# Four smaller input loads around the first weight columns, two products in token halves, and a re-made instruction order

## The chip, the cores and the metric

The kernel runs on one core of one Trainium2 chip. The metric is device time in microseconds (us), the median of three runs. A profile of one execution is also given; its span runs from the first to the last instruction, and its device time contains some 1.7 us more than the span.

## The reference

The input x has 2048 tokens of 512 bf16 values. Two branches are computed from it and mixed by a gate that depends on the token:

```python
def _A_ref(x, wqkv, wo):          # 32 heads of 16, window W = 256
    q, k, v = qkv[0], qkv[1], qkv[2]
    scores = jnp.einsum("bhqd,bhkd->bhqk", q, k) * (Dh ** -0.5)
    mask = (idx[:, None] - idx[None, :] >= 0) & (idx[:, None] - idx[None, :] < W)
    p = _softmax(jnp.where(mask[None, None], scores, -1e9), axis=-1)
    return o_of(p, v) @ wo
...
def _B_ref(x, w1, w3, w2):        # F = 1376
    return (_silu(x @ w1) * (x @ w3)) @ w2
...
g = _sigmoid((x * gate_w).sum(-1, keepdims=True))
return g * a + (1 - g) * b
```

`o_of` stands for the product of the probabilities with v. So there is a sliding-window attention with its four projections, a gated feed-forward network, and the mix.

## The kernel before

**Tiling.** Everything lies in on-chip memory. x is needed with its 512 features on the partitions: `xT`, in four feature blocks of 128, over 2048 tokens. Tokens are worked in four blocks of 512 (`tcb` or `tq`, 0 to 3). The attention takes the heads in four groups of eight (`c`, 0 to 3). For each group and each key tile of 128 tokens, `main_batch` makes scores with matmuls that use 32 rows of the array each, four beside each other (line 661, "row form"); `edge_batch` does the same for the parts of the window at the edges (line 711). ScalarE takes the exponential (lines 665 and 715), GpSimd cuts it to the window (lines 670, 675 and 728), and `pv` multiplies by v with matmuls that use 32 columns each, four beside each other (line 801, "column form"). All other matmuls use the whole array ("full form"): the q, k and v projections (lines 553 and 606), w1 and w3 (line 967), w2 (line 1026, and line 1082 for the last 128 tokens), and the output projection (line 1055).

**The opening.** The function `opening` (line 422) writes the start out by hand. `constants` makes the identity. `warm_up(WARM)` (line 420) sends 30 matmuls on constants, whose results nobody reads. Then loads are issued on two queues, SyncE's (SP) and ScalarE's (ACT): x's tokens 0 to 255 on SP, tokens 256 to 511 on ACT (line 394), then w1's first 256 columns, half of the rows on SP and half on ACT (line 406). After a table load and `gate_w` on ACT, SP goes on with the first columns of k, w3, q and v, then more of w1 and w3. The remaining three quarters of x come as transposing loads (`turn_x`, line 399) on SP, in order between the later weights.

The first 512 tokens are turned on TensorE instead: four tiles of 128 tokens, four transposes each (line 493), evicted to `xT` by VectorE for tiles 0, 1 and 3 (line 498) and by ScalarE for tile 2 (line 500). A short `warm_up(2)` is planned with the turns. Then the first product of w1 (f = 0, 128 of the 1376 columns, token block 0) runs in two token halves (lines 997 and 999): its first half needs tiles 0 and 1 alone, its second half tiles 2 and 3 too. The k and q projections of the first block are split in the same way (lines 560 and 561). Every other w1 product, f = 1 among them, waits for all four tiles, and also for `last_up`, which is the w3 product of the f before it (line 994).

**The order.** After the opening, the order of all instructions is made by a planner at build time. Each piece of work is an `add(engine, duration, function, dependencies, due, ...)`. `Plan.emit` runs a simulation with these durations: it takes the engine that can start first and, of what could start there, the piece with the smallest due time. The order in which the pieces are taken is the order in which the instructions are written into the engines' queues. At run time each engine goes through its queue in that order and waits where an input is late. The due times come from a table `K` of some 25 numbers (`T0`, `TA`, `PV`, `SEP` and so on) plus a number for each piece, `SHIFT[n]`, where n counts the calls of `add`. The constants `landed` (line 453) tell the planner when each early load will have arrived. Two further numbers in `K`, `ADJ` and `SEP`, change the due times of work in row or column form, depending on the form that TensorE is in.

There are four single PSUM banks (`ch`) for full-form and column-form work, and one block of four banks (`su`) for the scores.

Of the kernel before, what the change touches and what calls it, by code (L numbers as in the profile page):

```python
# [262 lines left out]
def kernel(  # L263
# [12 lines left out]
    nc = tc.nc  # L276
# [17 lines left out]
    VW = DH + 1  # L294
    HALF = (0, 1, 2, 3, 4)
    SCALE = float(DH) ** -0.5
    WARM = 30

    pp = ctx.enter_context(tc.tile_pool(name="pp", bufs=1))
    ps = ctx.enter_context(tc.tile_pool(name="ps", bufs=1, space=bass.MemoryType.PSUM))  # L300
# [47 lines left out]
    add = plan.add  # L348
# [113 lines left out]
    x_in = [arrive(u) for u in landed["x"]]  # L462
# [671 lines left out]
```

## Time and profile before

| | |
|---|---|
| device time, median of 3 runs | 235.06 us |
| the three runs | 234.85, 235.06, 235.82 us |
| device time of the profiled execution | 235.33 us |
| its span | 233.6 us |
| TensorE busy (share of the span) | 225.2 us (96%) |
| VectorE busy | 181.7 us (78%) |
| ScalarE busy | 181.9 us (78%) |
| GpSimd busy | 152.8 us (65%) |
| data moved by DMA | 11.57 MB |

In the rows, PE is TensorE's matmul side and PEld its weight loads, DVE is VectorE, ACT is ScalarE, POOL is GpSimd, and SPq and ACTq are the DMA queues of SyncE and ScalarE. A row of the timeline has its start and its length in us, then engine, line and operation, the tile written and the tile read, and in brackets the idle time before it with what ended it. Rows that follow each other closely are merged, with "x8" for eight of them. Matmuls overlap: one with 512 columns is shown some 380 ns long, though the next starts earlier than that; what a matmul costs is therefore read from the starts.

### The profile page before, as it was taken

The numbers are of one execution on the slowest core, as the hardware profiler recorded it, in microseconds if no ns is written. First come the engines' busy times: TensorE is split into PE (matmuls) and PEld (weight loads), VectorE is DVE, ScalarE is ACT, GpSimd is POOL, SyncE is SP. The second block draws the span as 40 slices with busy tenths as digits, with TensorE's granted clock in tenths as the row PEclk, the third lists the DMA queues.
The fourth block names the chain that finished last, engine by engine and source line by source line (L and its number), as shares of the span: only waits on it lengthen the run. The fifth ranks groups of instructions, "written<-read, shape, count | busy, mean of one in ns | idle before, by whom it ended". The sixth has DMA issues, their size and how long they took to land.

```text
span 233.6 us, 8254 instructions
## 1 busy us (share of the span) xinstructions
PE 225.2 (96%) x3596; PEld 115.9 (50%) x3635; DVE 181.7 (78%) x317; ACT 181.9 (78%) x165; POOL 152.8 (65%) x245
## 2 busy tenths in 40 slices
PE   7999999999999999999999999999999999999995
PEld 7545545634544345545547353535444355455543
DVE  5457777993798869987878787887986779997864
ACT  3479999797778998878998989887968998867310
POOL 7135999576877964749865869567679856654300
DMA  6997701800004000000003000000000000140202
GB/s 188 322 183 196 93 1 21 225 27 1 6 4 133 3 11 14 3 3 3 4 12 81 25 1 3 3 3 0 4 3 3 0 3 18 34 145 20 91 7 84
DMA packets 20653, 11.57 MB, mean 50 GB/s; under 512 B 10025, under 2 KB 20617, under 8 KB 20617
## 3 DMA queue, kind: packets, MB, share of 16 engines
q1 hardware_dynamic: 19920, 10.62, 19.5%
q8 instruction: 28, 0.46, 0.8%
q10 hardware_dynamic: 696, 0.43, 0.6%
q14 instruction: 9, 0.07, 0.1%
HBM read 6.85 MB, written 2.10 MB: 38 GB/s over the span
## 4 chain that ended last, share of the span: by engine, by line
PE 89%; DMA 4%; SPq 2%; issue 2%; DVE 2%
PE ch L967 30%; PE ch L1026 16%; PE ch L553 11%; PE ch L801 9%; PE su L661 8%; PE ch L606 6%; PE ch L1055 6%; PE su L711 2%; DMA xT<-in_A_x_dram 2%; SPq L399 2%; DMA xs<-in_A_x_dram 2%; PE ch L1082 1%; PE ch L904 1%; SPq L406 1%; DVE bsb L1030 0%
## 5 line engine op out<-in xcount | busy, mean ns | idle before, releaser
L665 ACT ACTIVATE Em<-su 128x2048 bf16<-128x2048 f32 x60 | 112.7, 1878 | 22.5 <-PE su L661 20.9
L967 PE MATMUL ch<-xT,w_sb 128*128 128x512 bf16 (+1 forms) x304 | 77.0, 377 | 2.7 <-issue 1.7
L675 POOL TENSOR_SCALAR_AFFINE_SELECT Em<-Em 64x512 bf16<-64x512 bf16 x56 | 37.8, 674 | 26.2 <-ACT Em L665 24.5
L670 POOL TENSOR_SCALAR_AFFINE_SELECT Em<-Em 64x512 bf16<-64x512 bf16 x60 | 40.5, 676 | 18.0 <-ACT Em L665 16.0
L728 POOL TENSOR_SCALAR_AFFINE_SELECT Ee<-Ee 64x1024 bf16<-64x1024 bf16 x32 | 39.5, 1233 | 11.4 <-ACT Ee L715 10.3
L967 PEld LDWEIGHTS <-w_sb 128*128 128x128 bf16 x324 | 28.7, 98 | 32.8 <-issue 4.7
L981 DVE SCALAR_TENSOR_TENSOR h<-tt,ch 128x512 bf16<-128x512 bf16 (+1 forms) x44 | 29.7, 679 | 12.9 <-ACT tt L977 12.6
L1026 PE MATMUL ch<-w_sb,hT 128*128 128x512 bf16 x143 | 37.0, 380 | 0.8 <-issue 0.6
L553 PE MATMUL ch<-xT,wqkv_sb 128*128 128x512 bf16 (+1 forms) x126 | 33.5, 367 | 0.6 <-issue 0.3
L715 ACT ACTIVATE Ee<-su 128x2048 bf16<-128x2048 f32 x16 | 30.1, 1880 | 5.0 <-PE su L711 5.0
L642 POOL COPY vs<-vs 64x256 bf16<-64x256 bf16 x64 | 28.9, 452 | 7.5 <-DVE vs L630 3.1
L987 DVE SCALAR_TENSOR_TENSOR hT<-h,ch 128x512 bf16<-128x512 bf16 x40 | 27.1, 682 | 5.4 <-PE ch L967 3.3
L977 ACT ACTIVATE tt<-ch 128x512 bf16<-128x512 f32 (+1 forms) x44 | 26.1, 598 | 3.9 <-PE ch L967 3.1
L801 PEld LDWEIGHTS <-vs 128*17 128x17 bf16 x1664 | 20.5, 92 | 5.8 <-issue 4.5
L801 PE MATMUL ch<-Em,vs 128*17 128x256 bf16 (+2 forms) x672 | 22.6, 242 | 0.0
L801 PE MATMUL ch<-Ee,vs 128*17 128x64 bf16 x992 | 22.1, 193 | 0.0
L1026 PEld LDWEIGHTS <-hT 128*128 128x128 bf16 x150 | 13.5, 98 | 16.4 <-issue 2.5
L553 PEld LDWEIGHTS <-wqkv_sb 128*128 128x128 bf16 x136 | 12.0, 97 | 13.3 <-issue 2.7
L606 PE MATMUL ch<-wqkv_sb,xT 128*128 128x256 bf16 x128 | 17.2, 273 | 0.2 <-issue 0.2
L661 PE MATMUL su<-qT,kz 32*128 32x256 bf16 x240 | 17.3, 278 | 0.0
L661 PE MATMUL su<-qT,k 32*128 32x256 bf16 x240 | 16.6, 268 | 0.0
L661 PEld LDWEIGHTS <-kz 32*128 32x128 bf16 x240 | 6.0, 91 | 21.2 <-issue 20.8
(83 smaller groups left out, 251.9 us busy)
## 6 DMA issues: line engine op xcount, KB each, us to landing
out_dram<-ot SPq DMA_DIRECT2D x15, 128.0 KB, 1.7
wqkv_sb<-in_A_wqkv_dram SPq DMA_DIRECT2D x6, 256.0 KB, 4.5
w_sb<-in_B_w_dram SPq DMA_DIRECT2D x2, 608.0 KB, 4.8
w_sb<-in_B_w_dram SPq DMA_DIRECT2D x3, 384.0 KB, 3.8
w_sb<-in_B_w_dram SPq DMA_DIRECT2D x2, 512.0 KB, 6.5
wo_sb<-in_A_wo_dram SPq DMA_DIRECT2D x4, 128.0 KB, 3.2
xs<-in_A_x_dram ACTq DMA_DIRECT2D x1, 256.0 KB, 3.8
xs<-in_A_x_dram SPq DMA_DIRECT2D x1, 256.0 KB, 3.5
```

The source lines that it names most:

```text
L553: nc.tensor.matmul(pst[:, t0:t1], lhsT=wqkv_sb[:, dc, col + c * P:col + (c + 1) * P], rhs=xT[:, dc, tq * 512 + t0:tq * 512 + t1], start=(d ...
L606: nc.tensor.matmul(ch[vj.at["ch"]][:, (m - m0) * 2 * P:(m - m0 + 1) * 2 * P], lhsT=xT[:, dc, m * P:(m + 1) * P], rhs=wqkv_sb[:, dc, 2 * D ...
L661: nc.tensor.matmul(su[:, s, a * 256:(a + 1) * 256], lhsT=head_keys(r, t, a), rhs=qT[r, q0:q0 + 256], start=True, stop=True)
L665: nc.scalar.activation(out=Em[job.at["Em"]][:], in_=su[:].rearrange("p s (a q) -> p s a q", a=2), func=ACT.Exp, scale=SCALE)
L670: nc.gpsimd.affine_select(out=e, in_=e, pattern=[[0, 8], [1, KB]], compare_op=ALU.is_ge, fill=0.0, base=0, channel_multiplier=-1)
L675: nc.gpsimd.affine_select(out=e, in_=e, pattern=[[0, 8], [-1, KB]], compare_op=ALU.is_ge, fill=0.0, base=-1, channel_multiplier=1)
L715: nc.scalar.activation(out=Ee[ej.at["Ee"]][:].rearrange("p s t k q -> p s (t k q)"), in_=su[:], func=ACT.Exp, scale=SCALE)
L728: nc.gpsimd.affine_select(out=e, in_=e, pattern=[[0, 4], [0, 4], [1, KB]], compare_op=ALU.is_ge, fill=0.0, base=0, channel_multiplier=-1)
L801: nc.tensor.matmul(po[32 * s:32 * s + VW, lo - 512 * w:hi - 512 * w], lhsT=vs[:, i, a * VW:(a + 1) * VW], rhs=mov, start=(n == 0), stop=(n ...
L967: nc.tensor.matmul(ch[job.at["ch"]][:, t0:t1], lhsT=wA[:, dc, :] if joint else w[:, dc, f * P:(f + 1) * P], rhs=xT[:, dc, tcb * 512 + t0:t ...
L981: nc.vector.scalar_tensor_tensor(out=h1[job.at["h1"]][ru, :], in0=tt[job.at["tt"]][rg, :], scalar=1.0, in1=ch[job.at["ch"]][rg, :], op0=AL ...
L1026: nc.tensor.matmul(bps[:], lhsT=ht[:, mm * P:(mm + 1) * P], rhs=w2_sb[0:fs, f, :], start=(f == 0), stop=(f == NFC - 1))
```

## The change

Loads of x: four of one tile each (128 KB). Tiles 0 and 1 come first, on SP and ACT, then w1's first columns on both queues, then tiles 2 and 3 on both. The 30 matmuls of the warm-up become 23. The product of w1 with f = 1 in token block 0 is now also made in two token halves, and it no longer depends on the w3 product of f = 0. The planner is given other landing times for the early loads, and other durations for the turns (0.43 us for the first two tiles, 0.23 us for the others, in place of 0.36 us for each).

All numbers in `K` are replaced, and the whole of `SHIFT` too. As f = 1 is two calls of `add` in place of four, the list has 1516 numbers in place of 1518. The median size of a number in it is 6.1 in place of 45.3. What the order of the instructions is after this is not to be read from the diff: it comes out of the planner.

```diff
 SHIFT = [
-    0, 0, 0, 0, 0, 0, 0, 0, 0, 0, 0, 0, 0, 0, 0, 0, 0, 143.67, 103.37, 60.03, 88, 142.21, 38.94, 42.12, -2.51, 57.41,
...
+    1.81, 79.34, 55.8, 47.5, 3.69, 40.28, 95.35, 10.12, -10.19, -9.12, 8.12, 0, 0.19, 12.25, 5.26, 32.25,
 ]
...
-    WARM = 30
+    WARM = 23
...
-    K = {"T0": 1.021, "TA": 175.674, "TF0": -5.614, "TF1": 219.201, "PV": -22.302, "EDGE": -2.04, "HOLD": -6.16, "LEAD": -1.713, "QLEAD": -2.523, "V": 9.16, "O0": 9.293, "O1": -5.39, "O2": 6.658, "O3": 32.037, "FE": 0.855, "PE": 8.645, "VE": -2.133, "MK": 65.837, "UP": 4.276, "_km": 1.0, "_lo": 1.0, "LE": 1.877, "ADJ": 7.677, "SEP": -19.643, "BE": 5.555, "OE": 1.299, "END": 5.842}
+    K = {"T0": 2.597, "TA": 171.79, "TF0": -2.088, "TF1": 212.023, "PV": -31.637, "EDGE": -1.998, "HOLD": -4.505, "LEAD": -3.245, "QLEAD": -5.562, "V": 7.957, "O0": 10.94, "O1": -1.559, "O2": 13.899, "O3": 33.228, "FE": 3.405, "PE": 4.943, "VE": -3.088, "MK": 50.721, "UP": 7.032, "_km": 1.0, "_lo": 1.0, "LE": -0.98, "ADJ": 3.157, "SEP": -29.885, "BE": 7.725, "OE": 8.717, "END": 4.513}
...
-        load_x(0, 2, nc.sync)
-        load_x(2, 4, nc.scalar)
+        load_x(0, 1, nc.sync)
+        load_x(1, 2, nc.scalar)
         load_w(w1_sb, B_w1, 0, 2 * P, True)
+        load_x(2, 3, nc.sync)
+        load_x(3, 4, nc.scalar)
...
-    landed = {"x": [3.6, 3.6, 4.4, 4.4, 14.5, 20.6], "w13": [5.25, 7.45, 10.8, 16.6, 12.2, 18.8],
-              "qkv": [6.5, 8.3, 9.1], "gw": 8.0}
+    landed = {"x": [3.65, 3.8, 5.5, 5.8, 14.5, 20.8], "w13": [4.6, 7.7, 10.8, 16.6, 12.2, 18.8],
+              "qkv": [6.85, 8.6, 9.45], "gw": 8.0}
...
-        a = add("PE", 0.36, tr, [x_in[m]], 0.1 * m, take=[(job, "ch")])
+        a = add("PE", 0.43 if m < 2 else 0.23, tr, [x_in[m]], 0.1 * m, take=[(job, "ch")])
...
-            if tcb or f:
+            if tcb or f > 1:
                 a = plan.pieces(HALF, 0.2155, lambda lo, hi, half=half, job=job: half(job, w1_sb, lo, hi),
                                 xt_ready[tcb] + win + last_up + (w_ab if joint else []), due, [(job, "ch")])
             else:
```

191 rows, old and new, of the table SHIFT are left out of this document.

## The prediction

> **What bounds the kernel now.** I read the page's busy shares and its chain of waits first, then the timeline of TensorE (PE), then the opening closely.
>
> ```profile
> span 233.6 us, 8254 instructions
> ...
> PE 225.2 (96%) x3596; PEld 115.9 (50%) x3635; DVE 181.7 (78%) x317; ACT 181.9 (78%) x165; POOL 152.8 (65%) x245
> ...
> PE 89%; DMA 4%; SPq 2%; issue 2%; DVE 2%
> ```
>
> PE is busy 96% of the span and holds 89% of the chain. The order of work matters only as far as it makes PE wait, or makes it change its form. What PE's time consists of shows where steps are followed by starts:
>
> ```profile
> 50.94 2.33 PE L1026 MATMUL ch<-w_sb,hT 128*128 128x512 bf16 x10
> 53.20 0.29 PE L661 MATMUL su<-qT,kz 32*128 32x256 bf16 x4
> 53.32 0.28 PE L661 MATMUL su<-qT,k 32*128 32x256 bf16 x4
> 53.53 0.82 PE L1026 MATMUL ch<-w_sb,hT 128*128 128x512 bf16 x2
> ...
> 20.81 0.41 PE L711 MATMUL su<-qT,kz 32*128 32x64 bf16 x32
> 21.15 0.61 PE L606 MATMUL ch<-wqkv_sb,xT 128*128 128x256 bf16 x4
> ...
> 22.25 1.47 PE L606 MATMUL ch<-wqkv_sb,xT 128*128 128x256 bf16 x12
> ...
> 195.00 0.21 PE L801 MATMUL ch<-Em,vs 128*17 128x64 bf16 x4
> ...
> 196.33 0.20 PE L801 MATMUL ch<-Ee,vs 128*17 128x64 bf16 x4
> 196.46 0.29 PE L661 MATMUL su<-qT,kz 32*128 32x256 bf16 x4
> ...
> L967 PEld LDWEIGHTS <-w_sb 128*128 128x128 bf16 x324 | 28.7, 98 | 32.8 <-issue 4.7
> L967 PE MATMUL ch<-xT,w_sb 128*128 128x512 bf16 (+1 forms) x304 | 77.0, 377 | 2.7 <-issue 1.7
> ```
>
> Ten w2 matmuls and what lies around them: one is shown 0.38 long, so the step is (2.33 - 0.38)/9 = 0.217 us, and ten take 2.17. The row batch starts 2.26 after the first, so 0.09 to 0.10 goes into the change of form. The batch holds PE 0.33 until the next full matmul; 0.33 less some 0.22 of streaming is a second change. I take 0.105 a change. A matmul with 256 columns costs (1.47 - 0.27)/11 = 0.109. A column group takes 1.36 (195.00 to 196.33 and 0.03 for the last), then 0.10 to the row batch beside it.
>
> The loops give the counts: 336 matmuls of 512 columns for w1 and w3, 176 for w2 (the last 11 in parts), 128 for k and q, 64 for the output: 704 x 0.217 = 152.8. 128 for v at 0.109 are 14.0; the tail columns of line 904 about 2.0; 60 row batches at 0.22 are 13.2; 16 edge batches (20.81 to 21.15, less one change) at 0.24 are 3.8; 16 column groups 20.2 (those at the ends of the window are shorter). Together 206.0. In the timeline I count 172 changes of form: 76 row batches and 17 column stretches would have 186, but 14 times a row batch stands beside a column group, as at 196.46, and one change is saved. 172 x 0.105 = 18.1. The sum is 224.1.
>
> ```profile
> 5.58 1.07 PE L967 MATMUL ch<-xT,w_sb 128*128 128x256 bf16 x8
> ...
> 230.56 0.22 PE L1082 MATMUL ch<-w_sb,hX 96*128 96x128 bf16 x1
> ```
>
> From the first product at 5.58 to the last at 230.6 there are 225.0 us. So **at most about 1 us of waiting is left** between them. The waits of 0.16 that the groups put down to "issue" are mostly no waits: line 967 has 324 weight loads but 304 matmuls, so the record of a first matmul is missing where the idle time is shown. Outside lie 5.58 us of opening and some 3 us of last eviction and store, which the change leaves.
>
> **The opening now.**
>
> ```profile
> 0.82 0.46 SPq L394 DMA_DIRECT2D xs<-in_A_x_dram  x1
> ...
> 6.42 6.68 SPq L399 DMA_TRANSPOSE xT<-in_A_x_dram  x4
> ...
> SPq L406 <- DMA xs<-in_A_x_dram: 1.2, 1, 1.2
> ...
> xs<-in_A_x_dram ACTq DMA_DIRECT2D x1, 256.0 KB, 3.8
> xs<-in_A_x_dram SPq DMA_DIRECT2D x1, 256.0 KB, 3.5
> ...
> 1.50:3.30 1.80, 1.80 (x20) 1.80 (x18) 1.58 (x4) 1.41 (x2) 1.58 (x9) 1.00 0.67 151
> 1.50:4.00 2.50, 2.50 (x26) 2.35 (x23) 1.87 (x5) 1.49 (x2) 2.17 (x12) 1.00 0.79 212
> 1.50:4.85 3.35, 3.04 (x35) 2.86 (x33) 1.94 (x6) 1.49 (x2) 2.96 (x14) 1.00 0.87 236
> ...
> 0.85 3.17 PE L420 MATMUL su<-const-bfloat16-1.0 128*128 128x128 bf16 x30 [0.85 <-PEq L1118]
> ...
> 4.34 0.62 PE L493 MATMUL ch<-ident,xs 128*128 128x128 bf16 x8 [0.31 <-DMA xs<-in_A_x_dram]
> 4.78 1.21 DVE L498 COPY xT<-ch 128x512 bf16<-128x512 bf16 x3 [1.15 <-PE ch L493]
> 5.33 0.59 ACT L500 COPY xT<-ch 128x512 bf16<-128x512 bf16 x1 [1.96 <-PE ch L493]
> 6.80 1.04 PE L553 MATMUL ch<-xT,wqkv_sb 128*128 128x256 bf16 x8 [0.15 <-issue]
> 7.68 1.03 PE L967 MATMUL ch<-xT,w_sb 128*128 128x512 bf16 x4
> 8.54 1.25 PE L553 MATMUL ch<-xT,wqkv_sb 128*128 128x256 bf16 x9
> ```
>
> x lands at 4.3 (SP) and 4.6 (ACT), and its first half product starts 1.25 after the former. By 8.54 three products are done: w1 and w3 of f = 0, and k. The last number of a windows row is GB/s: 1.8 us at 151 are 272 KB by 3.30, 2.5 at 212 are 530 KB by 4.00, 3.35 at 236 are 791 KB by 4.85. Since x has 524 KB, a load is seen 0.3 to 0.65 us after its last byte moved.
>
> **The change, part by part.**
>
> *Loads.* The bytes come in the order 262 KB (tiles 0, 1), 262 KB (w1), 262 KB (tiles 2, 3). With the delay just found, tiles 0 and 1 are seen at 3.6 to 3.95, w1 at 4.3 to 4.65, tiles 2 and 3 at 5.15 to 5.5. The first half product then starts at 3.6 + 1.25 = 4.85 at best; at 3.95 and 0.2 more for a turn at the slow clock of the warm-up it is 5.4. I take 5.1, 0.48 earlier than now. It and the first half of f = 1, 0.44 each (the k row: eight halves in 0.88), fill PE to 6.0. Turns of tiles 2 and 3 come between or behind, then evictions of 0.42 on DVE and 0.59 on ACT: 1.0 to 1.35 after landing, so 6.15 to 6.85; I take 6.55. Second halves until 7.4, then k (0.88) until 8.3. Again three products are done, at 8.3 in place of 8.54: **-0.25 us**. The early bounds give 6.15 + 1.75 = 7.9, a gain of 0.6; the late ones 6.85 + 1.75 = 8.6 and 0.2 for k's load arriving behind, a loss of 0.3. The move gains little: tiles 2 and 3 pay for what tiles 0 and 1 win. I count the last of the three as worth its whole difference, since PE has work without a break afterwards.
>
> *Queues.* SP and ACT issue one load more each, 0.46 to 0.5. On SP k, w3 and q come that much later; the sixth load already stood 1.2 waiting for x, which covers it for v and everything behind, the transposing loads at 6.42 among them. If that cover fails, the 0.5 reaches the second token block's data. On ACT the table load and `gate_w` move by 0.5; ACT's first eviction is at 5.33, so nothing waits. Cost 0; bounds 0 and 0.5.
>
> *Warm-up.* Seven fewer matmuls lie beside the loads and save nothing, PE waits for x there. *f = 1 in halves*: 0.88 for 0.87, **+0.01**; its four further weight loads lie beside matmuls (PEld is 50% busy).
>
> *Order.* Nothing in the trace shows the new one. Bounds: the 1 us of waiting can go, and a column group can have a row batch on both sides (34 contacts for 14, 20 x 0.105 = 2.1), so -3.1. On the other side all 14 contacts lost are +1.5, and waits can grow by, say, the 0.15 seen before the k product at 6.80, at each of the 16 column groups: 2.4, together +3.9. Contacts I take as they are. Waits can fall by 1 and rise without such a floor, so I take **+0.4**, nearer to the present 1 us than to the far end.
>
> The sum is 235.33 (profiled) - 0.25 + 0.01 + 0.4 = 235.5. The profiled execution lay 0.27 above the median of 235.06, so I forecast **235.2 us**.
>
> *The clock.* The granted clock reads 1.00 in every window above, yet the durations tell more:
>
> ```profile
> L420 PEld LDWEIGHTS <-const-bfloat16-1.0 128*128 128x128 bf16 x24 | 2.5, 144 | 0.8 <-issue 0.8
> ...
> L493 PEld LDWEIGHTS <-xs 128*128 128x128 bf16 x16 | 0.9, 98 | 0.5 <-DMA xs<-in_A_x_dram 0.5
> ```
>
> Before 3.2 a weight load took 144 ns, from 4.1 on 98; the warm-up's steps of some 0.107 halve only for the last few of the 30, near 3.6. Twenty-three such steps end at about 3.3, ahead of that moment. The Trainium skill ("TensorE: Matmul & The Clock Gate", Part 1) says that the array starts at half clock and that release takes about 3.4 us of sustained activity, in time and not in matmuls; the trace agrees in kind, with some 2.75 us from the first matmul. By that rule the shorter warm-up may miss its window; what this does is the third rival.
>
> **The rivals.**
>
> 1. *The order is tighter* (22%). With 8 more contacts (-0.84), half the waiting gone (-0.5) and the opening's -0.25 the time is 233.5. For it: the search had fresh numbers everywhere. Against: only 1 us is left to win in waits.
> 2. *Column groups ahead of their masks* (30%), the slower side. `pv` needs the last row batch's scores, its exponential and its mask:
>
> ```profile
> 216.30 0.29 PE L661 MATMUL su<-qT,kz 32*128 32x256 bf16 x4
> ...
> 216.75 1.88 ACT L665 ACTIVATE Em<-su 128x2048 bf16<-128x2048 f32 x1 [1.68 <-PE su L661]
> 218.69 0.66 POOL L670 TENSOR_SCALAR_AFFINE_SELECT Em<-Em 64x512 bf16<-64x512 bf16 x1 [1.20 <-ACT Em L665]
> 219.11 0.21 PE L801 MATMUL ch<-Em,vs 128*17 128x64 bf16 x4
> ```
>
>    Here the column group starts 2.8 after the batch, with its mask just in time. PE goes through its queue in order, so a group placed sooner holds up everything. 0.13 at each of 16 groups is 2.1 us, and 235.06 - 0.25 + 2.1 = 236.9. It decides from 0.09 a group (1.43 in all, 1.18 above the median). For it: `PV` and `SEP` make these groups due earlier, -31.6 for -22.3 and -29.9 for -19.6. Against: the planner places nothing before its inputs are planned ready.
> 3. *The change doesn't bring the first products forward* (10%): the clock stays low through them for a second stretch of 2.75, to 6.35. Both first halves take near double, second halves start at some 7.5, three products are done at 9.3, 0.75 late. With the order's 0.4 that is 236.2, half of this case on either side of the border.
>
> **How the numbers follow.** My forecast has 38%. A measurement of this kernel tells about 0.5% from no change, that is 233.9 to 236.2. Faster is the first rival, 0.22; slower the second and half the third, 0.35; the forecast and the rest are 0.43. The likeliest case alone holds 234.2 to 236.2; the range 233.3 to 237.2 takes in the rivals' times.
>
> **What would show it.** Right: the first w1 matmul near 5.1, second halves near 6.55, PE ending 225 us after its start, 172 changes give or take five. Wrong: line 420 weight loads staying at 144 ns and line 493's too (the clock); a first row of line 801 with idle time ahead of it and GpSimd as its releaser (second rival); clearly fewer changes of form (first).

## The result and the profile after

The changed kernel takes 237.45 us (median of 6 runs, 236.90 to 238.94), the kernel before, run beside it, 235.17 us (6 runs, 234.85 to 235.88). The ratio is 1.0104, with an interval of 1.0066 to 1.0141: about 1% slower, where 235.2 and a range up to 237.2 were forecast. The profiled execution took 237.75 us.

From its page, the busy shares:

```profile
span 236.0 us, 8308 instructions
...
PE 230.2 (98%) x3632; PEld 116.5 (49%) x3632; DVE 184.7 (78%) x317; ACT 181.7 (77%) x165; POOL 153.6 (65%) x245
```

TensorE seems 5 us busier, 98% for 96%. That is not a cause: the page of before lacks 39 matmul records (3596 beside 3635 weight loads), and a matmul that is followed at once by another overlaps it. The starts have to be read. The last matmul starts at 232.92, in place of 230.56: 2.36 us later.

**The opening.** TensorE's timeline of the changed kernel (start and length in us, line, tiles, idle time before):

```profile
3.60 1.03 PE L480 MATMUL ch<-ident,xs 128*128 128x128 bf16 x8
4.43 0.42 PE L405 MATMUL su<-const-bfloat16-1.0 128*128 128x128 bf16 x2
5.15 0.73 PE L954 MATMUL ch<-xT,w_sb 128*128 128x256 bf16 x4 [0.30 <-DVE xT L485]
6.14 0.65 PE L480 MATMUL ch<-ident,xs 128*128 128x128 bf16 x8 [0.26 <-DMA xs<-in_A_x_dram]
6.63 0.60 PE L954 MATMUL ch<-xT,w_sb 128*128 128x256 bf16 x4
7.21 1.03 PE L540 MATMUL ch<-xT,wqkv_sb 128*128 128x256 bf16 x8
8.08 0.60 PE L954 MATMUL ch<-xT,w_sb 128*128 128x256 bf16 x4
8.61 0.17 PE L502 MATMUL ch<-ident,gwr 4*128 4x4 bf16 x1
8.72 1.55 PE L954 MATMUL ch<-xT,w_sb 128*128 128x256 bf16 x8
```

The first product starts at 5.15, close to the forecast. But one half product (4 matmuls) later TensorE stands still, until tiles 2 and 3 arrive for their turns at 6.14. Four half products for w1 and k follow, the one at 6.63 still a first half: tile 3 is evicted only at 7.25. The sixth half, which makes three products, begins at 8.72 and is done four matmuls of 0.109 later, at 9.16. Without the small gate product at 8.61, which the kernel before makes only at 9.94, that is 9.05. Before, three products were done at 8.54. So the opening loses 0.5 us.

The pieces of the chain of waits show what TensorE waited for, and the table of DMA issues gives the times from issue to landing:

```profile
1.74 4.61 DMA xs<-in_A_x_dram
...
10.20 5.82 DMA xT<-in_A_x_dram
```

```profile
wo_sb<-in_A_wo_dram SPq DMA_DIRECT2D x4, 128.0 KB, 2.7
xs<-in_A_x_dram SPq DMA_DIRECT2D x2, 128.0 KB, 3.6
xs<-in_A_x_dram ACTq DMA_DIRECT2D x2, 128.0 KB, 4.6
```

Tile 3 was issued at 1.74 and was there at 6.35; 5.15 to 5.5 was forecast. By 4.85 us 828 KB had moved (3.35 us at 247 GB/s), more than the forecast's 791 KB, but by then only 493 of the 512 packets of x had started; the last one of tile 3 ended at 5.79. The first weights of k landed 0.55 later than before (7.08 for 6.53), and TensorE waited some 0.15 for them. The transposing load of the next 512 tokens landed at 16.02 (15.92 before), and there the new order holds a k product that needs it:

```profile
15.11 0.59 PE L540 MATMUL ch<-xT,wqkv_sb 128*128 128x512 bf16 x2
16.07 0.38 PE L540 MATMUL ch<-xT,wqkv_sb 128*128 128x512 bf16 x1 [0.37 <-DMA xT<-in_A_x_dram]
```

Two matmuls cost 0.43, so of the 0.96 between the starts 0.53 is a wait. The kernel before waits at this landing too, for 0.22: its matmul at 15.96 starts 0.44 after the one ahead.

**Two waits for VectorE.** The timelines of several engines near 115 and near 220:

```profile
113.26 2.43 POOL L715 TENSOR_SCALAR_AFFINE_SELECT Ee<-Ee 64x1024 bf16<-64x1024 bf16 x2 [0.98 <-ACT Ee L702]
...
114.60 1.36 DVE L725 TENSOR_TENSOR Ee<-Ee,mlast 128x512 bf16<-128x512 bf16 x1
...
115.66 0.82 PE L540 MATMUL ch<-xT,wqkv_sb 128*128 128x512 bf16 x3
...
115.88 0.74 DVE L1017 TENSOR_SCALAR bsb<-ch,omg 128x512 bf16<-128x512 f32 x1
...
116.67 0.60 PE L593 MATMUL ch<-wqkv_sb,xT 128*128 128x256 bf16 x4 [0.19 <-DVE bsb L1017]
...
217.82 2.43 POOL L715 TENSOR_SCALAR_AFFINE_SELECT Ee<-Ee 64x1024 bf16<-64x1024 bf16 x2 [1.50 <-ACT Ee L702]
...
219.16 1.36 DVE L725 TENSOR_TENSOR Ee<-Ee,mlast 128x512 bf16<-128x512 bf16 x1
...
220.22 0.61 PE L1069 MATMUL ch<-w_sb,hT 128*128 128x128 bf16 x8
...
220.45 0.74 DVE L1046 SCALAR_TENSOR_TENSOR ot<-ch,gq,bsb 128x512 bf16<-128x512 f32 x1
...
221.24 0.21 PE L788 MATMUL ch<-Em,vs 128*17 128x64 bf16 x4 [0.40 <-DVE ot L1046]
```

TensorE wants to begin a new product in a `ch` bank, and waits for VectorE to have read the bank's last content (lines 1017 and 1046 are named as releasers). VectorE comes late, because ahead of that in its queue stands line 725, the second mask of a last edge batch, which takes 1.36 us. It starts 0.13 after the second of GpSimd's two masks there (line 715). From 115.66 to 116.67 stand three matmuls of 0.217, so 1.01 - 0.65 = 0.36 is lost. The second wait is 0.48 (from 220.22 to 221.24 are 1.02; the same eight matmuls and the change of form take 0.54 in the experiment below where VectorE is in time). Together 0.84.

The same instruction in both kernels, all four executions of it with shortest, median and longest time in ns (first row after, second row before):

```profile
L725 DVE TENSOR_TENSOR Ee<-Ee,mlast x4: 411/884/1360, 72.9 to 219.2; 128x512 bf16<-128x512 bf16 x4
```

```profile
L738 DVE TENSOR_TENSOR Ee<-Ee,mlast x4: 411/614/1360, 64.4 to 217.7; 128x512 bf16<-128x512 bf16 x4
```

It took 1.36 us once before as well (at 64.43, 0.30 after a mask of GpSimd had started), and no row of TensorE shows a wait behind it. In these rows it is not enough that the other engine works beside it; what differs is which starts first. In the changed kernel near 73 us VectorE started 0.02 ahead; it took 0.41, and the mask of GpSimd took 0.91, where most of that line take 0.65. Near the end of the kernel before it fell behind GpSimd's mask and took 0.41 too. Two rows of the changed kernel, then two of the kernel before:

```profile
72.94 0.41 DVE L725 TENSOR_TENSOR Ee<-Ee,mlast 128x512 bf16<-128x512 bf16 x1
72.96 0.91 POOL L662 TENSOR_SCALAR_AFFINE_SELECT Em<-Em 64x512 bf16<-64x512 bf16 x1 [0.21 <-ACT Em L652]
...
216.35 1.15 POOL L728 TENSOR_SCALAR_AFFINE_SELECT Ee<-Ee 64x1024 bf16<-64x1024 bf16 x1
...
217.69 0.41 DVE L738 TENSOR_TENSOR Ee<-Ee,mlast 128x512 bf16<-128x512 bf16 x1
```

**Changes of form.** Counted in the timeline as before: 175 for 172 (11 contacts of row batch and column group for 14), 3 x 0.105 = 0.3 us.

**One wait without a name.** Inside an edge batch:

```profile
45.70 0.41 PE L698 MATMUL su<-qT,kz 32*128 32x64 bf16 x31
46.44 0.20 PE L698 MATMUL su<-qT,kz 32*128 32x64 bf16 x1 [0.33 <-issue]
46.57 0.60 PE L954 MATMUL ch<-xT,w_sb 128*128 128x512 bf16 x2
```

The batch takes 0.87 to the next full matmul, where 0.34 is usual. No semaphore is named. Whether this belongs to the change is a question for the experiments.

### The profile page after: what moved, and what is told of

It reads as the page before. It is cut to its first block, busy times and chain, and to the rows that moved or that the text cites. A ratio compares the mean times of both kernels' runs of the same rounds, so it can differ in the third digit from the quotient of the medians.

```text
span 236.0 us, 8308 instructions
## 1 busy us (share of the span) xinstructions
PE 230.2 (98%) x3632; PEld 116.5 (49%) x3632; DVE 184.7 (78%) x317; ACT 181.7 (77%) x165; POOL 153.6 (65%) x245
## 4 chain that ended last, share of the span: by engine, by line
PE 89%; DMA 4%; DVE 2%; SPq 2%; ACT 1%; issue 1%; ACTq 0%
PE ch L954 30%; PE ch L1013 15%; PE ch L540 11%; PE ch L788 9%; PE su L648 8%; PE ch L1042 6%; PE ch L593 5%; DMA xT<-in_A_x_dram 2%; PE su L698 2%; DMA xs<-in_A_x_dram 2%; SPq L384 1%; PE ch L891 1%; PE ch L1069 1%; ACT Em L652 1%; DVE bsb L1017 1%
## 5 line engine op out<-in xcount | busy, mean ns | idle before, releaser
L954 PE MATMUL ch<-xT,w_sb 128*128 128x512 bf16 (+1 forms) x328 | 80.4, 376 | 0.3 <-DVE xT L485 0.3
L715 POOL TENSOR_SCALAR_AFFINE_SELECT Ee<-Ee 64x1024 bf16<-64x1024 bf16 x32 | 40.3, 1258 | 12.5 <-ACT Ee L702 11.3
L954 PEld LDWEIGHTS <-w_sb 128*128 128x128 bf16 x328 | 29.3, 98 | 33.7 <-issue 6.1
L1013 PE MATMUL ch<-w_sb,hT 128*128 128x512 bf16 x150 | 38.4, 380 | 0.0
L629 POOL COPY vs<-vs 64x256 bf16<-64x256 bf16 x64 | 28.3, 442 | 13.8 <-DVE vs L603 8.6
L540 PE MATMUL ch<-xT,wqkv_sb 128*128 128x512 bf16 (+1 forms) x136 | 34.0, 367 | 0.4 <-DMA xT<-in_A_x_dram 0.4
L1017 DVE TENSOR_SCALAR bsb<-ch,omg 128x512 bf16<-128x512 f32 x15 | 11.2, 746 | 8.6 <-PE ch L1013 8.5
```

What stands on the lines that cost most here:

```text
L540: nc.tensor.matmul(pst[:, t0:t1], lhsT=wqkv_sb[:, dc, col + c * P:col + (c + 1) * P], rhs=xT[:, dc, tq * 512 + t0:tq * 512 + t1], start=(d ...
L715: nc.gpsimd.affine_select(out=e, in_=e, pattern=[[0, 4], [0, 4], [1, KB]], compare_op=ALU.is_ge, fill=0.0, base=0, channel_multiplier=-1)
L954: nc.tensor.matmul(ch[job.at["ch"]][:, t0:t1], lhsT=wA[:, dc, :] if joint else w[:, dc, f * P:(f + 1) * P], rhs=xT[:, dc, tcb * 512 + t0:t ...
L1013: nc.tensor.matmul(bps[:], lhsT=ht[:, mm * P:(mm + 1) * P], rhs=w2_sb[0:fs, f, :], start=(f == 0), stop=(f == NFC - 1))
```

## The experiments

The expectations say themselves what each of their theories holds. Each group of runs has its own runs of the kernel before beside it on the same chip.

**1. The loads alone, the order alone.** The kernel before with the new loads and 23 warm-up matmuls, its order untouched:

```diff
-    WARM = 30
+    WARM = 23
-        load_x(0, 2, nc.sync)
-        load_x(2, 4, nc.scalar)
+        load_x(0, 1, nc.sync)
+        load_x(1, 2, nc.scalar)
         load_w(w1_sb, B_w1, 0, 2 * P, True)
+        load_x(2, 3, nc.sync)
+        load_x(3, 4, nc.scalar)
```

> The kernel before with the four-piece loads and 23 warm-up matmuls alone; its planner's numbers, and so its order, stay. Theory A (the new loads are a loss by themselves, and the end moves by what the opening loses): TensorE's queue has the turns of tiles 2 and 3 ahead of the first product, they land near 6.1 us in place of 4.6, so the first product starts near 6.6 in place of 5.58 and the end is 0.9 to 1.1 us later, about 236.2. Rival B (the opening has slack, the loss is all in the order behind it): the end moves by less than 0.3 us.

Measured: 237.3 us (235.74 to 238.87, 10 runs) beside 235.12 (21 runs), ratio 1.0088 [1.0058, 1.0118]. The timeline of TensorE:

```profile
6.20 0.62 PE L495 MATMUL ch<-ident,xs 128*128 128x128 bf16 x8 [1.33 <-DMA xs<-in_A_x_dram]
6.66 1.29 PE L969 MATMUL ch<-xT,w_sb 128*128 128x256 bf16 x8
```

In the old order all turns stand ahead of the first product, so the late tiles 2 and 3 delay it from 5.58 to 6.66. The new loads with the short warm-up are a loss by themselves; in the opening the halves of f = 1 and the new order win part of it back. Theory A's 236.2 fits the profiled execution (236.09, its last matmul 0.74 later than before) and not the median: the 23 warm-up matmuls, run 5, are part of this run. What the loads cost without them no run shows alone.

The reverse, the changed kernel with the old loads and 30 warm-up matmuls:

> The changed kernel with x in two pieces ahead of w1 and 30 warm-up matmuls again; order and halves as in the changed kernel. Theory A: the wait of 0.42 us ahead of the turns of tiles 2 and 3 goes, the first product starts near 5.6 in place of 5.15, the last of the four halves ends about 0.4 earlier; but the wait for the transposed load near 16 us grows by most of that, so the end is 0.1 to 0.4 earlier than the changed kernel. Rival B: no difference. Rival C (the loads are the whole loss): back to within 0.5 us of the kernel before.

Measured: 236.87 us (236.50 to 237.73, 6 runs), ratio 1.0076 [1.0055, 1.0097]. Both waits for VectorE are in its trace, 0.36 and 0.48. So most of the loss is there without the new loads: **it lies in the order.** The two halves of the change don't add up (2.18 and 1.75 against 2.28 together), since either one by itself already makes the start late: tiles 2 and 3 are turned at 6.20 in the one and at 6.03 in the other, for 4.91 before.

**2. The bank waits.** The changed kernel, with the two masks of a last edge batch made in one instruction, from a tile that holds both patterns:

```diff
+    mfull = pp.tile([P, 4, KB], BF16, name="mfull")
...
-            full = 2 if last else 4
...
-            if last:
-                e = Ee[ej.at["Ee"]][:, :, 2:4, 1, :]
...
+            mb = (mfull[:][:, None, :, :].to_broadcast([P, 4, 4, KB]) if last
+                  else medge[:, 1][:, None, None, :].to_broadcast([P, 4, 4, KB]))
+            nc.vector.tensor_tensor(out=e, in0=e, in1=mb, op=ALU.min)
```

> The changed kernel with VectorE's masks of the last edge batch of each head group joined into one instruction, from a mask tile made in the opening; the order stays. In the changed kernel's profile the second of the two instructions took 1.36 us in two of four cases, and VectorE then freed a PSUM bank late for TensorE near 116 and 221 us (waits of 0.35 and 0.47). Theory A (the loss is a sum of separate waits): both waits go or shrink, the end is 0.5 to 0.8 us earlier than the changed kernel. Rival D (the waits are symptoms of a pace set elsewhere, and TensorE loses the time again further on): the two waits go, but the end moves by less than 0.2 us.

Measured: 236.01 us (235.47 to 238.04, 12 runs), ratio 1.0046 [1.0028, 1.0065]; the last matmul starts at 231.10. The timeline near 220:

```profile
217.22 1.00 DVE L728 TENSOR_TENSOR Ee<-Ee,mfull 128x1024 bf16<-128x1024 bf16 x1
...
218.15 0.74 DVE L1048 SCALAR_TENSOR_TENSOR ot<-ch,gq,bsb 128x512 bf16<-128x512 f32 x1
...
218.94 0.61 PE L1071 MATMUL ch<-w_sb,hT 128*128 128x128 bf16 x8
...
219.48 0.21 PE L790 MATMUL ch<-Em,vs 128*17 128x64 bf16 x4
```

One instruction of 1.00 replaces 0.73 and 1.36, VectorE frees its bank in time, and both waits are gone. The median falls by 1.44 us, more than the 0.84 seen in the trace; the intervals of the two ratios (1.0066 to 1.0141, and 1.0028 to 1.0065) leave room for the difference. Since both kernels run the same order, their matmuls can be set side by side. The last one is 1.82 earlier than in the first profile of the changed kernel: 0.41 of it is there by 16 us, 0.52 comes in the edge batch near 46 that is shown above, and 0.36 and 0.48 at the two waits. The latter two are the repair; the others vary from one execution to the next (run 7).

**3. The wait for the second token block.** Four matmuls of the k product near 15 moved behind a score batch and two matmuls of w3:

```diff
+        grp = [r for r in order if r[1].seq in (73, 74, 75, 76)]
+        order[:] = [r for r in order if r[1].seq not in (73, 74, 75, 76)]
+        i = [r[1].seq for r in order].index(828) + 1
+        order[i:i] = grp
```

> The changed kernel with the four matmuls of one projection of the second token block, which wait 0.53 us near 16 us for the transposed load, placed behind a score batch and two matmuls of w3. Theory A: the wait goes, everything behind is about 0.5 us earlier, the end 0.4 to 0.5 us earlier. Rival D: the wait goes, the step comes back at a later wait and the end moves by less than 0.2 us.

Measured: 237.16 us (236.62 to 237.43, 6 runs), ratio 1.0081 [1.0061, 1.0101]. The 0.53 is gone, but in the timeline the score batch behind it now waits for ScalarE's exponential instead:

```profile
15.37 0.29 PE L652 MATMUL su<-qT,kz 32*128 32x256 bf16 x4 [0.32 <-ACT Em L656]
```

The last matmul starts at 232.13, as in the further executions of the changed kernel (232.11 and 232.24, run 7). This wait covers another; it is not a cost that can be taken out alone.

**4. The repairs together.** The changed kernel with the old loads, 30 warm-up matmuls, one mask, and the first half product of f = 1 moved behind the turns of tiles 2 and 3:

```diff
+        grp = [r for r in order if r[1].seq in (813,)]
...
+        i = [r[1].seq for r in order].index(41) + 1
+        order[i:i] = grp
```

> The changed kernel's order with x in two pieces and 30 warm-up matmuls, the edge mask in one instruction, and the turns of tiles 2 and 3 ahead of the first product again. new_order_old_loads ended 1.67 us behind the kernel before in the profiles: 0.83 are the two waits for a bank, 0.45 the turns inside, 0.3 three more changes of form. Theory A (separate waits, nothing comes back): 1.67 - 0.83 - 0.45 = 0.4 us above the kernel before, 235.3 to 235.8. Rival D (lost again further on): 236.3 or more.

Measured: 235.59 us (235.31 to 236.89, 12 runs) beside 235.38 (28 runs), ratio 1.0020 [1.0004, 1.0036]. The timeline:

```profile
5.10 0.61 PE L488 MATMUL ch<-ident,xs 128*128 128x128 bf16 x8
5.64 1.03 PE L958 MATMUL ch<-xT,w_sb 128*128 128x256 bf16 x8
```

The turns of tiles 2 and 3 stand at 5.10 again, and the first two half products follow without a break. With the repairs the new order is nearly as good as the old one: in its profiled execution the last matmul starts at 230.58, 0.02 later than before. It still has the 175 changes of form, 0.3 more, but three products are done at 8.35, counted without the gate product as above (0.19 earlier than before), and the landing of the second token block is no longer waited for. No run tried the changes of form alone. Nothing in it beats the kernel before.

**5. The warm-up.** The kernel before with `WARM = 23`, with nothing else changed:

> The kernel before with 23 warm-up matmuls in place of 30, nothing else. In the profiles so far the last weight load at half clock lies between 3.6 and 5.5 us and the runs with the new loads scatter over 2 to 3 us (before: 1). Theory E (with TensorE less busy in the first microseconds, its clock opens a stretch later in some executions): the median rises by 0.3 to 1.0 us and the runs scatter over more than 1.5 us. Rival F (the scatter comes from the landings of the four pieces, the warm-up has cover): the median stays within 0.3 us of the kernel before and the runs within about 1 us.

Measured: 236.65 us (234.86 to 237.59, 10 runs), ratio 1.0045 [1.0018, 1.0073]. A term that I had put at nothing costs 1.27 us in the median, and the runs lie 2.7 us apart where those of the kernel before lie 1.5 apart. The profiled execution was a short one, 235.26. With 8 warm-up matmuls:

> The kernel before with 8 warm-up matmuls: TensorE is idle from about 1.9 to 4.3 us. Theory E: the last weight load at half clock (over 130 ns) lies at 6 us or later in the profile, and the median is 1 to 2.5 us above the kernel before, since each microsecond at half clock costs half of one. Rival F: the clock opens as before and the end moves by less than 0.3 us.

Measured: 237.09 us (235.84 to 237.96, 12 runs) beside 235.41 (20 runs), ratio 1.0066 [1.0043, 1.0088]. The last weight load at half clock starts at 7.61 in its profile, so theory E holds on both counts. With 30 in the changed kernel:

> The changed kernel with 30 warm-up matmuls in place of 23, nothing else. Theory E (too little work in the first microseconds lets the clock open a stretch later in some executions): the median falls by 0.5 to 1.0 us from 237.45 and the scatter of 2.0 shrinks towards 1.2, though tiles 0 and 1 are now turned only when the warm-up ends, near 4.05. Rival F (23 is enough here, since the order has products between): no change, or 0.1 to 0.4 slower by the later turns.

Measured: 237.13 us (236.46 to 237.86, 6 runs), ratio 1.0077 [1.0051, 1.0102], not to be told from the changed kernel's 1.0104 [1.0066, 1.0141]. In its profile tiles 2 and 3 landed at 5.60 and 5.81, but were turned only at 6.39, behind a half product that still ran at the slow clock; the last slow weight load starts at 6.39. So 30 warm-up matmuls don't open the clock by 3.6 in every kernel, and no run shows what the shorter warm-up costs the changed kernel: its three profiles have the last slow weight load at 5.32, 5.25 and 4.42.

More warm-up work, in two places. The new loads with the old order, 26 matmuls ahead and 26 in place of 2 between the turns:

> The order before with the four-piece loads as in old_order_new_loads, but with TensorE kept busy while it waits for tiles 2 and 3: 26 warm-up matmuls first and 26 in place of 2 behind the turns of tiles 0 and 1. Theory E: the scatter shrinks to about 1 us and the median falls from 237.3 to 235.8 to 236.2, which is what its profiled run shows (the last matmul 0.74 later than before). Rival F: scatter and median stay near 237.3.

Measured: 236.62 us (236.14 to 238.18, 7 runs), ratio 1.0061 [1.0036, 1.0086]. Neither theory holds: the median falls by less than E says, and the runs still lie 2.0 apart. In its profile tiles 2 and 3 landed at 5.10 and 5.41, early enough; but the 26 matmuls hold TensorE from 4.43 until the turns begin at 6.15, and the first product starts at 6.60. The fillers took the time that the late landing cost in run 1. The kernel before with 33 and four more behind the turns:

> The kernel before with 33 warm-up matmuls and four more behind the turns of tile 3, which fill TensorE's gaps at 4.0 and 5.35 us; nothing else. Theory E: the scatter shrinks and the median is 0.1 to 0.4 us below the kernel before; if the clock is already open in time there, the same within 0.2. Rival F: the fillers delay the turns and the first product and the end is 0.1 to 0.3 later.

Measured: 236.19 us (235.63 to 237.47, 9 runs), ratio 1.0037 [1.0013, 1.0060]. This missed: full clock came by 4.5, but its execution has two waits inside edge batches, again without a name:

```profile
45.63 0.29 PE L713 MATMUL su<-qT,kz 32*128 32x64 bf16 x14 [0.32 <-issue]
...
62.65 0.20 PE L713 MATMUL su<-qT,k 32*128 32x64 bf16 x2 [0.55 <-issue]
```

**6. All of x first.** The kernel before with x in four pieces, all ahead of w1:

```diff
-        load_x(0, 2, nc.sync)
-        load_x(2, 4, nc.scalar)
+        load_x(0, 1, nc.sync)
+        load_x(1, 2, nc.scalar)
+        load_x(2, 3, nc.sync)
+        load_x(3, 4, nc.scalar)
```

> The kernel before with x in four pieces, all four ahead of w1, order and 30 warm-up matmuls as before. Tiles 0 and 1 are then seen near 3.6 and turned as the warm-up ends at 4.05, tiles 2 and 3 near 4.6, w1 as now near 5.25: the first product starts near 5.3 in place of 5.58. Theory A (the end follows the opening): 0.1 to 0.3 us faster than before, if tiles 2 and 3 land as early as now. Rival G (each further load delays what is behind it on SyncE's queue): k and w3 land 0.5 later, and the gain is lost: within 0.2 of before or up to 0.4 slower.

Measured: 236.01 us (235.41 to 236.53, 12 runs), ratio 1.0025 [1.0012, 1.0038]. The first two tiles are turned from 4.0 on, but the weight loads stay at the slow clock until 5.6, and the first product waits for w1 until 6.25, as w1 lands at 6.21 for 5.23 before. What x gains w1 loses.

**7. The same kernels again.** To tell waits of the order from waits of one execution, and to catch longer executions of the short warm-up in a profile, two kernels were profiled twice more.

> The changed kernel itself, another profiled execution. In its first profile TensorE lost 0.52 us inside an edge batch at 45.9 us with nothing named as the releaser, and waited 0.35 at 116 and 0.47 at 221. Theory A: the latter two are there again, the former is not. If the clock decides (theory E), executions above 238 show a last weight load at half clock later than 6 us.

> As after_again_1: one more execution of the changed kernel, to see which waits belong to the order and recur, and which belong to the execution.

Measured: 236.90 and 237.06 us, beside 235.42 for one run of the kernel before; the last matmul starts at 232.11 and 232.24. From the timeline of the first of them:

```profile
45.28 0.53 PE L698 MATMUL su<-qT,kz 32*128 32x64 bf16 x32
45.75 0.61 PE L954 MATMUL ch<-xT,w_sb 128*128 128x512 bf16 x2
...
115.85 1.03 PE L593 MATMUL ch<-wqkv_sb,xT 128*128 128x256 bf16 x8 [0.20 <-DVE bsb L1017]
...
220.43 0.21 PE L788 MATMUL ch<-Em,vs 128*17 128x64 bf16 x4 [0.41 <-DVE ot L1046]
```

The two waits for VectorE are there again, 0.36 and 0.48 in both. The edge batch near 45.5 takes 0.47 and 0.35 in place of 0.87, so its 0.52 belonged to one execution; the kernel before has 0.48 for its batch at 45.27. The wait for the second token block was 0.07 in one and 0.52 in the other. None was above 238, so what makes the longest executions of the changed kernel (238.66, 238.94) stays open.

> The kernel before with 23 warm-up matmuls, another profiled execution. Its ten runs lie between 234.9 and 237.6 and its one profile is of a fast one (235.26). Theory E: an execution above 236.5 shows weight loads at half clock until 7 us or later. Theory H (waits inside batches, with nothing named): it shows such a wait of 0.5 or more instead, and the clock open by 6.

> As warm23_again_1: one more execution of the kernel before with 23 warm-up matmuls, so that a slow one may be among the profiled ones.

Measured: 236.22 and 237.51 us. The weight loads of the opening in the three executions of this one kernel (the 235.26 of run 5, then 236.22, then 237.51), of which eight take some 0.85 at full clock and 1.5 at half:

```profile
5.92 0.39 PEld L967 LDWEIGHTS <-w_sb 128*128 128x128 bf16 x4
...
7.02 1.08 PEld L553 LDWEIGHTS <-wqkv_sb 128*128 128x128 bf16 x9
```

```profile
5.95 1.53 PEld L967 LDWEIGHTS <-w_sb 128*128 128x128 bf16 x8
...
8.19 0.75 PEld L553 LDWEIGHTS <-wqkv_sb 128*128 128x128 bf16 x7 [0.28 <-issue]
```

```profile
6.07 1.54 PEld L967 LDWEIGHTS <-w_sb 128*128 128x128 bf16 x8
...
8.30 1.43 PEld L553 LDWEIGHTS <-wqkv_sb 128*128 128x128 bf16 x7 [0.27 <-issue]
```

By the single records the last weight load at half clock starts at 5.81, 7.77 and 10.01. The times differ by half of that: 1.95 later costs 0.96, 4.20 later costs 2.25. So with 23 warm-up matmuls **the clock opens at another time in each execution**, and this explains the differences between these three. The clock theory holds here; the 0.36 that the longest also waits at 50.5 for a load of w2 is a small part beside it.

## Why the prediction was wrong

**The order: the term was mis-sized.** I put +0.4 on it, inside bounds of -3.1 and +3.9. Its waits for a bank and its changes of form in the trace are 0.84 + 0.3 = 1.1 us, and the run with the order and the old loads measured +1.75. That run also turns tiles 2 and 3 later, at 6.03 for 4.9. The argument that "PE is 96% busy, so at most 1 us of waiting is left" limits what a new order can win, and says nothing of what it can lose. The floor was used as if it were a scale.

**The opening: the sign was wrong.** I had three products done at 8.3, 0.25 earlier; they were done at 9.05, 0.5 later. The step that failed is the landing of tiles 2 and 3: I read it off the bytes moved, as if the loads were served one after the other. The bytes were right (828 KB by 4.85, for 791), but packets of later loads were among them, and the last packet of tile 3 ended at 5.79. How late that is differs: in the eight profiles with this order of loads tile 2 landed between 5.10 and 6.16, and in one alone, that with fillers in run 5, was it there as early as forecast. The first product at 5.15 was right (5.1), and from the landing of tile 3 to the end of its eviction (7.25) 0.9 passed, near the 1.0 to 1.35 forecast. The queues' cost of 0 held for the transposing load (16.02 for 15.92), but not for the first weights of k: TensorE waited 0.15, 0.18 and 0.37 for them in the three profiles.

**The warm-up: 0 was wrong in itself**, 1.27 us in the kernel before, though in the changed kernel no difference between 23 and 30 could be told. I had seen that 23 steps end at 3.3, ahead of the moment at which the clock opened (3.6), and left it to a rival of 10% instead of pricing it in the sum.

**The second rival came nearest, with the wrong releaser.** It had a column group that holds up TensorE, and 236.9. There is one, at 221. It waits for a PSUM bank from VectorE, not for GpSimd's mask, it is one of 16 and not all of them, and it costs 0.48 and not 0.13. The other wait is of a v projection. The third rival's first half products ran at the slow clock until 5.32, not 6.35.

**The signs named in advance.** First w1 matmul near 5.1: yes. Changes of form 172 give or take five: yes, 175. Second halves near 6.55: no; the product at 6.63 is a first half, and the second halves follow from some 7.65 (k) and 8.08 (w1). PE ending 225 us after its start: no, 232.9 - 5.15 = 227.8.

**The account.** In the first profile of the changed kernel the last matmul starts 2.36 later than before, in the two further ones 1.55 and 1.68. All three have 0.84 for the banks and 0.3 for the changes of form. The opening adds 0.5, 0.55 and 0.36. The wait for the second token block is 0.53, 0.07 and 0.52, for 0.22 before, and the edge batch near 45 us takes 0.87, 0.47 and 0.35, for 0.48 before. That makes 2.3, 1.5 and 1.7. The sums fit; that the parts simply add is an assumption, since run 3 shows a wait that only made room for the next, and a wait of some 0.16 near 56 us in all three is not counted.

## What to carry to other kernels

When an order is made anew for an engine that is 96% busy, what it can lose has no floor: look for the instruction that takes several times as long when another engine has started first (here 1.36 us for 0.41), and for the buffer that is freed behind it in its queue. If another load shares the queues, place the user of a load by a measured landing and not by bytes. And price a shorter warm-up, even one that only shortens a wait: 23 for 30 cost the kernel before 1.27 us. More was no gain either: 33 and four more measured 0.78 above it.

## What of the hardware was not expected

A piece of 128 KB issued at 1.74, behind 128 KB of w1 on its queue, took 4.61 us to land; four loads of 128 KB of wo in the same kernel took 2.7 in the median. In three profiles of the changed kernel the turns of tiles 2 and 3 began at 6.14, 6.17 and 5.78, each within 0.05 of tile 2's landing.

The same VectorE instruction took 0.41 us alone, 0.41 when it started 0.02 ahead of a mask of GpSimd, which then took 0.91, and 1.36 when it started 0.13 to 0.30 after one. Both waits of TensorE stood behind one of 1.36.

The clock opened at 5.8, 7.8 and 10.0 us in three executions of one kernel with 23 warm-up matmuls; with 30 the profile of the kernel before had it open at 3.6, but that of run 6 (all of x first) and that of the changed kernel with 30 (run 5) only at 5.6 and 6.4. The Trainium skill ("TensorE: Matmul & The Clock Gate", Part 1) says that the activity window is free-running, some 3.4 us long, and that its phase at the start differs from run to run. The traces agree in kind; their spread of 4.2 us is wider than one such window.

Inside the edge batch near 45 us TensorE lost up to 0.5 us with no releaser named, in one execution and not in the next, in both orders. Its cause was not tried.
